# Where the softmax sums of the memory rows are formed, and which engines copy the second half of the values

## The chip, the core and the metric

The kernel runs on one core of a Trainium2 chip. The metric is the device time in microseconds (us) of one execution, as a median over runs. The engines are TensorE (PE, with its weight loads shown apart as PEld), VectorE (DVE), ScalarE (ACT), GpSimd (POOL) and SyncE (SP, which issues transfers).

## The reference, cut to what matters

The network is A, B, A, B with residuals and layer norms. A is attention with a recurrent memory, B a gated MLP with a mixing matrix over tokens. The change lies in A:

```python
for s in range(n_seg):                        # 2048 tokens in 64 segments of 32
    h = concat([mem, xs], axis=1)             # 8 memory rows + 32 token rows
    q, k, v = h @ Wq, h @ Wk, h @ Wv          # 32 heads of 128
    p = softmax(where(mask, q @ k.T * scale, -1e9))
    o = (p @ v) @ Wo
    mem = o[:, :8]                            # carried to the next segment
    outs.append(o[:, 8:])
```

Each segment needs the memory that the one before it made, so the 64 segments of a block follow each other. All 12 inputs come in bfloat16.

## The kernel before, in words

`a_block` runs one attention block and is called twice, so there are 128 segments in all. Its nested function `segment` emits one segment; the order of PE, DVE and ACT instructions is the order in which the code writes them (`manual_schedule`), and each engine works through its own list in that order. The framework adds the semaphores between engines. Where the code knows that two accesses don't touch each other, it says so itself (`declare_no_dep`, in `other_bank` and in `fold`).

The 32 heads are worked in two halves, r = 0 and r = 1, of 16 heads. In PSUM a tile of 128 partitions x 2 x 512 floats fills two banks. The tiles `att`, `attO[0]` and `attO[1]` are such pairs of banks; `accA` and `accB` are single banks. In the course of a segment they hold different things under different names:

- `att` holds psQ, then the scores psS of both halves, then psT, the sums over the softmax of the token rows.
- `attO[0]` holds psK and the first half's values, then psO[0]: the outputs of half 0 before they are normalised (columns 0 to 319 of each bank).
- `attO[1]` holds psO[1]: the outputs of half 1 (columns 0 to 319), sums in columns 320 to 383, and pw, the second part of the output projection, in columns 384 to 511.
- `accB` holds psV (the second half's values, psW in the code), then px, the first part of the output projection.

The stretch around the change, in the order of the code (lines of the profile):

1. `v_mm(1, ...)` (L762) forms the values of half 1 in four steps of four matmuls, one for each quarter of the contraction. The scores of half 1 (L1113, L1117) stand after the second of them.
2. `exps` (L1122, ACT) writes S, and `close` (L1125, DVE) multiplies it by the mask into E, where the rows of the contraction are split in two groups g of 64 partitions.
3. `sums_zero` (L1136): 16 matmuls form the sums of half 0 for the 8 memory rows, in columns 224 to 351 of the scores' first bank. Each multiplies E by the constant `half`, whose ones cover one group of 64 rows, and writes 32 partitions; they stand between the third and the fourth value step.
4. `inverse(r)` on ACT takes the logarithm of such sums (L1179) and then exp of its negative (L1180), which gives 1/sum in Rm. For half 0, ACT's copy of the values from psV (L1226) stands between the two.
5. `fill()` puts in PE work that doesn't belong to the segment: products for the next block of 128 tokens, or parts of earlier output rows (here L964 or L762).
6. `pv(0)` (L1162, L1165) forms the outputs of half 0, `sums_tokens` (L1154) the sums for the token rows of both halves, `sums_one` (L1145) the memory sums of half 1 with four matmuls, and `pv(1)` the outputs of half 1. These use 64 rows and all 128 columns of the array.
7. `memory_out(0)` (L1183, DVE) multiplies the memory rows of psO[0] by Rm into uT for 16 heads. `spare1` puts in other DVE work, a second `fill()` other PE work.
8. `inverse(1)`, then `memory_out(1)` for the other 16 heads.
9. `wo_pairs` (L945) is the output projection of the first 16 heads into px, `wo_rest` (L952) that of the others into pw. From these the memory of the next segment is built (`fold`, L1049 on ACT and L1053 on DVE, `build_hA`, L1060 and L1062).

Of the kernel before, what the change touches and what calls it, by code (L numbers as in the profile page):

```python
# [7 lines left out]
BF16 = mybir.dt.bfloat16  # L8
# [6 lines left out]
P = 128  # L15
# [52 lines left out]
def _consts(ctx, tc, c, b_sp, between):  # L68
    nc = tc.nc
    cp = ctx.enter_context(tc.tile_pool(name="consts", bufs=1))  # L70
    bsp = cp.tile([P, 16], F32, name="bsp")
    tctx = ExitStack()
    tmp = tctx.enter_context(tc.tile_pool(name="consts_tmp", bufs=1))
    maskf = tmp.tile([P, 224], F32, name="maskf")
    nc.gpsimd.memset(maskf[:], 1.0)
    fourth = tmp.tile([P, 4, 32], F32, name="fourth")
    nc.gpsimd.memset(fourth[:], 0.0)
    nc.gpsimd.affine_select(out=fourth[:], in_=fourth[:], compare_op=ALU.not_equal, fill=1.0,
                            base=0, pattern=[[-1, 4], [-4, 32]], channel_multiplier=1)
    own = maskf[:, 160:224].rearrange("p (i q) -> p i q", i=4)  # L80
    is_own = tmp.tile([P, 4, 1], F32, name="is_own")
    nc.vector.tensor_reduce(out=is_own[:], in_=fourth[:], op=ALU.max, axis=mybir.AxisListType.X)
    nc.vector.tensor_copy(own, is_own[:].to_broadcast([P, 4, 16]))
    between()
    for q in range(0, P, 32):
        blk = maskf[q:q + 32, 0:160].rearrange("p (i q) -> p i q", i=4)[:, :, 8:32]
        nc.gpsimd.affine_select(out=blk, in_=blk, compare_op=ALU.is_ge, fill=0.0, base=8,
                                pattern=[[0, 4], [1, 24]], channel_multiplier=-1)
        last = own[q:q + 32, :, 8:16]
        nc.gpsimd.affine_select(out=last, in_=last, compare_op=ALU.is_ge, fill=0.0, base=0,  # L90
                                pattern=[[1, 4], [4, 8]], channel_multiplier=-1)
    maskN = cp.tile([P, 2, 224], BF16, name="maskN")
    nc.vector.memset(maskN[:], 0.0)
    for gs in range(4):
        nc.vector.tensor_copy(maskN[32 * gs:32 * gs + 32, gs % 2, :], maskf[32 * gs:32 * gs + 32, :])
    ones = cp.tile([P, P], BF16, name="ones")
    nc.vector.memset(ones[:], 1.0)
    half = cp.tile([P, 2, 32], BF16, name="half")
    nc.vector.memset(half[:], 0.0)
    for g in range(2):  # L100
        nc.vector.memset(half[64 * g:64 * g + 64, g, :], 1.0)
    bsp_bf = cp.tile([P, 16], BF16, name="bsp_bf")

    def load_bsp():
        nc.vector.memset(bsp_bf[:], 0.0)
        nc.sync.dma_start(bsp_bf[:], b_sp.rearrange("(t p) -> p t", p=P))
        return lambda: nc.vector.tensor_copy(bsp[:], bsp_bf[:])

    c["bsp"], c["load_bsp"] = bsp, load_bsp
    tctx.close()  # L110
    c.update(maskN=maskN, ones=ones, half=half)
    return c


# [510 lines left out]
def cols_rhs(w, j, kt, cg):  # L625
    at = 2048 * (j % 2) + 512 * cg
    return w[j // 2][:, kt, at:at + 512]
# [90 lines left out]
def a_block(tc, c, rows, front, MV_in, RS_in, MV_out, RS_out, ahead, wo, S, first):  # L718
    nc = tc.nc
    NSEG = S // SEG  # L720
    NB = S // P
    scale = float(DH) ** -0.5
    maskN, ones, half = c["maskN"], c["ones"], c["half"]

    with ExitStack() as ctx:

# [33 lines left out]
        def mm_chunk(ps, lhs, rhs, kts=range(KT)):  # L760

            return [nc.tensor.matmul(ps[32 * cg:32 * cg + 32, :], lhsT=lhs(kt, cg), rhs=rhs(kt, cg), start=(kt == 0), stop=(kt == KT - 1),  # L762
                                     tile_position=(0, 32 * cg)) for kt in kts for cg in range(4)]

        def other_bank(mms, *reads):

            for m in mms:
                for r in reads:
                    tc.declare_no_dep(m.ins, r.ins, reason="another bank of the tile")
# [300 lines left out]
        def segment(s, fill, spare1, spare2, spare3, tail, loads):  # L1070
# [4 lines left out]
            VA = vsp.tile([P, 2, 4, DH], BF16, name="VA")  # L1075
# [6 lines left out]
            E = segp.tile([P, 2, 2, 224], BF16, name="E", bufs=1)  # L1082
# [9 lines left out]
            def v_mm(r, ps, kts=range(KT)):  # L1092
                return mm_chunk(ps, lambda kt, cg: hA_cur[:, kt, :], lambda kt, cg: cols_rhs(w, 4 + r, kt, cg), kts)

            def ends(q):

                return q.rearrange("p h (b e) -> p h b e", e=8)[:, :, 0:5:4, :]
# [5 lines left out]
            def heads40(q):  # L1103
                return q.rearrange("p (i q) -> p i q", q=40)
# [16 lines left out]
            def exps(r):  # L1121
                return nc.scalar.activation(out=S[:, r], in_=psS[:, r, 0:224], func=ACT.Exp, scale=scale)  # L1122

            def close(r):
                nc.vector.tensor_tensor(out=E[:, r], in0=S[:, r].unsqueeze(1).to_broadcast([P, 2, 224]), in1=maskN[:], op=ALU.mult)  # L1125

            def e_all(e, lo, hi):

                return e[:, :, 0:160].rearrange("p n (i q) -> p n i q", q=40)[:, :, :, lo:hi]

            def e_own(e, b):
                return e[:, :, 160:224].rearrange("p n (i b e) -> p n i b e", i=4, b=2)[:, :, :, b, :]

            def sums_zero(pN):

                return [nc.tensor.matmul(pN[32 * cg:32 * cg + 32, 64 * g:64 * g + 64], lhsT=half[:, g, :], rhs=e_own(E[:, 0], 0) if k else e_all(E[:, 0], 0, 8),  # L1136
                                         start=False, stop=True, tile_position=(0, 32 * cg), skip_group_check=True)
                        for k in range(2) for g in range(2) for cg in range(4)]

            def sums_one():  # L1140

                for k in range(2):
                    for g in range(2):
                        e = E[64 * g:64 * g + 64, 1]
                        nc.tensor.matmul(psO[1][:, g, 320:384], lhsT=ones[64 * g:64 * g + 64, :], rhs=e_own(e, 0) if k else e_all(e, 0, 8),  # L1145
                                         start=(k == 0), stop=True, skip_group_check=True)

            def sums_tokens(ps):

# [7 lines left out]
            def pv(r):  # L1157

                for i in range(4):
                    for g in range(2):  # L1160
                        o = psO[r][:, g, 0:320].rearrange("p (s i q) -> p s i q", s=2, i=4)[:, :, i, :]
                        nc.tensor.matmul(o, lhsT=VA[64 * g:64 * g + 64, r, i, :], rhs=E[64 * g:64 * g + 64, r, :, 40 * i:40 * i + 40],  # L1162
                                         start=(r == 0 and i == 0), stop=True, skip_group_check=True)
                for g in range(2):
                    nc.tensor.matmul(ends(heads40(psO[r][:, g, 0:320])), lhsT=VX[64 * g:64 * g + 64, j4, r, :],  # L1165
                                     rhs=E[64 * g:64 * g + 64, r, :, 160:224], start=False, stop=True, skip_group_check=True)
# [10 lines left out]
            def inverse(r, src):  # L1177
                rm = Rm[:, r]
                nc.scalar.activation(out=rm, in_=src, func=ACT.Ln)  # L1179
                return lambda: nc.scalar.activation(out=rm, in_=rm, func=ACT.Exp, scale=-1.0)  # L1180

            def memory_out(r):
                nc.vector.tensor_tensor(out=hview(uT_cur[:], r, 24, 32), in0=oview(r, 0, 8), in1=Rm[:, r].rearrange("p g (n q) -> p g n q", q=8), op=ALU.mult)  # L1183
# [21 lines left out]
            psS = att.tile([P, 2, 512], F32, name="psS")  # L1205
            scores(0)
            expd = exps(0)
# [8 lines left out]
            psW = accB.tile([P, 512], F32, name="psV")  # L1216
            v_mm(1, psW, (0, 1))
            other_bank(scores(1), expd)
            expd = exps(1)
            v_mm(1, psW, (2,))  # L1220
            pN = psS[:, 0, 224:352]
            other_bank(sums_zero(pN), expd)
            v_mm(1, psW, (3,))
            Rm = segp.tile([P, 2, 2, 64], F32, name="Rm", bufs=1)
            invert = inverse(0, pN.rearrange("p (g q) -> p g q", g=2))
            nc.scalar.copy(VA[:, 1].rearrange("p i e -> p (i e)"), psW[:])  # L1226
            invert()
            close(1)

            psO = [attO[r].tile([P, 2, 512], F32, name="psO") for r in range(2)]  # L1230
            if not begin:
                fill()
            pv(0)
            psT = att.tile([P, 2, 512], F32, name="psT")
            sums_tokens(psT)
            sums_one()
            pv(1)
            memory_out(0)
            spare1(E)
            if not begin:  # L1240
                fill()
            inverse(1, psO[1][:, :, 320:384])()
            memory_out(1)
            run(copies)
            Rt = segp.tile([P, 2, 512], F32, name="Rt", tag="Rt", bufs=1)
# [57 lines left out]
        start = nc.vector if first else nc.gpsimd  # L1303
# [138 lines left out]
        for i in range(H // 2):  # L1442
            for k in range(4):
                h = 2 * i + k % 2
                nc.tensor.matmul(pw[32 * k:32 * k + 32, :], lhsT=ends[k // 2][:, h, :], rhs=wo.head(h).rearrange("p (kt g el) -> p g kt el", kt=4, g=4),
                                 start=(i == 0), stop=(i == H // 2 - 1), tile_position=(0, 32 * k))
# [46 lines left out]
```

## Time and profile before

| What | Value |
|---|---|
| Time, median of 3 runs | 1604.93 us (1603.9 to 1605.56) |
| Profiled execution: its own time | 1610.6 us |
| Profiled execution: its span, first to last instruction | 1608.9 us |
| Granted TensorE clock | 1.000 |
| PE busy | 1579.1 us (98%), 41021 matmuls |
| DVE busy | 1070.4 us (67%) |
| ACT busy | 1052.3 us (65%) |
| POOL busy | 306.5 us (19%) |

In the profile an instruction stands under the line that issued it, with output tile, input tile, partitions x elements, and a count where several are merged. A wait line names the engine and instruction that sat idle, then what released it, then the idle time in all, how often, and the longest.

### The profile page before, as it was taken

Reading aid. Unit: us, or ns where it says so; the run is one execution under the profiler, and the core shown is the slowest. Engines: PE = TensorE matmul, PEld = TensorE weight load, DVE = VectorE, ACT = ScalarE, POOL = GpSimd, SP = SyncE. Lnnn points to the kernel's source line nnn. Section 1 sums busy time; section 2 is a strip of 40 time slices with the busy share of each in tenths; the row PEclk is TensorE's granted clock in tenths of the full one; section 3 lists DMA queues with packets and bytes.
Section 4 is the critical chain, followed back from the end, with each engine's and each line's share of the span. In section 5 each row is a group of like instructions: output and inputs, shape, how many; then the busy total and the mean of one; then the engine's idle time right before and its main releaser. Section 6 shows DMA issues by size and latency. Waiting matters only on the chain.

```text
span 1608.9 us, 90911 instructions
## 1 busy us (share of the span) xinstructions
PE 1579.1 (98%) x41021; PEld 981.3 (61%) x41046; DVE 1070.4 (67%) x3066; ACT 1052.3 (65%) x2279; POOL 306.5 (19%) x674
## 2 busy tenths in 40 slices
PE   7899999999999999999999999999999999999999
PEld 3566666666666666666656666666666766665565
DVE  4667766677777776784466666666677667768622
ACT  4677777777777777670057777777777777776400
POOL 6211111112211221320011111111122122224000
PEclk9999999999999999999999999999999999999999
DMA  9322112222311332378952212212233223426698
GB/s 364 131 57 46 40 44 44 50 42 82 80 43 40 87 86 61 106 172 175 209 162 45 48 44 50 44 47 46 73 92 73 47 72 92 97 54 178 143 194 164
DMA packets 255773, 149.67 MB, mean 93 GB/s; under 512 B 188504, under 2 KB 231104, under 8 KB 255384
## 3 DMA queue, kind: packets, MB, share of 16 engines
q1 hardware_dynamic: 241464, 97.68, 27.4%
q0 software_dynamic: 13920, 46.18, 8.9%
q8 instruction: 321, 5.26, 1.4%
q14 instruction: 68, 0.56, 0.1%
HBM read 60.21 MB, written 39.55 MB: 62 GB/s over the span
## 4 chain that ended last, share of the span: by engine, by line
PE 92%; DMA 5%; issue 1%; DVE 1%; ACT 1%; POOL 1%; SPq 0%; POOLq 0%; DVEq 0%; ACTq 0%
PE psQ L762 13%; PE psK L762 13%; PE psb L762 9%; PE pg L403 9%; PE psO L952 7%; PE px L945 7%; PE psm L762 7%; PE psV L762 7%; PE pwB L964 3%; PE psO L1162 3%; PE pz L302 3%; PE py L446 2%; PE psT L1154 2%; PE psS L1113 2%; DMA Wk_sb<-in_A_Wk_dram 1%
## 5 line engine op out<-in xcount | busy, mean ns | idle before, releaser
L762 PEld LDWEIGHTS <-hT 128*32 128x32 bf16 x12288 | 345.3, 96 | 259.2 <-DVE hT L1062 17.7
L762 PE MATMUL psV<-Wv_sb,hT 128*32 128x512 bf16 x2048 | 166.4, 379 | 0.0
L1087 ACT CAST rows<-psQ 128x512 bf16<-128x512 f32 x256 | 145.4, 588 | 23.2 <-PE psQ L762 19.4
L1183 DVE TENSOR_TENSOR uT<-psO,Rm 128x128 bf16<-128x128 f32 x256 | 74.6, 291 | 123.6 <-ACT Rm L1180 123.4
L1090 DVE STREAM_TRANSPOSE QQ<-rows 128x256 f32<-128x256 f32 x256 | 112.5, 439 | 66.2 <-ACT rows L1087 63.6
L1122 ACT ACTIVATE S<-psS 128x224 bf16<-128x224 f32 x256 | 92.2, 360 | 98.1 <-PE psS L1117 98.1
L1090 DVE STREAM_TRANSPOSE KA<-rows 128x256 f32<-128x256 f32 x256 | 113.0, 441 | 64.9 <-ACT rows L1087 62.4
L403 PE MATMUL pg<-z,wspT 128*128 128x344 bf16 x1024 | 154.3, 309 | 0.0
L762 PE MATMUL psK<-Wv_sb,hT 128*32 128x512 bf16 x2048 | 153.2, 378 | 0.0
L1186 DVE TENSOR_TENSOR uT<-psO,Rt 128x384 bf16<-128x384 f32 x256 | 139.9, 547 | 16.4 <-ACT Rt L1265 14.4
L1265 ACT ACTIVATE Rt<-Rt 128x512 f32<-128x512 f32 x256 | 147.3, 622 | 4.0
L952 PE MATMUL psO<-Wo_high,uT 128*32 128x128 bf16 x8192 | 143.0, 219 | 4.1 <-issue 2.2
L762 PE MATMUL psQ<-Wq_sb,hT 128*32 128x512 bf16 x2048 | 136.4, 379 | 0.2 <-issue 0.2
L762 PE MATMUL psQ<-Wk_sb,hT 128*32 128x512 bf16 x2048 | 136.2, 379 | 0.0
L762 PE MATMUL psK<-Wk_sb,hT 128*32 128x512 bf16 x2048 | 136.0, 379 | 0.0
L762 PE MATMUL psm<-Wq_sb,hT 128*32 128x512 bf16 x2048 | 136.0, 379 | 0.0
L945 PE MATMUL px<-Wo,uT 128*32 128x256 bf16 x3840 | 133.8, 273 | 1.3 <-issue 1.2
L952 PEld LDWEIGHTS <-uT 128*32 128x32 bf16 x8192 | 123.6, 97 | 16.2 <-issue 7.8
L403 PEld LDWEIGHTS <-wspT 128*128 128x128 bf16 x1024 | 100.1, 98 | 53.4 <-issue 0.4
L1262 ACT ACTIVATE Rt<-psT 128x1024 f32<-128x1024 f32 x127 | 130.1, 1024 | 3.1
L945 PEld LDWEIGHTS <-uT 128*32 128x32 bf16 x4096 | 104.5, 97 | 25.2 <-issue 2.6
L1044 POOL COPY KX<-old 128x128 bf16<-128x128 bf16 x128 | 65.5, 539 | 263.8 <-PE psS L1117 170.7
(224 smaller groups left out, 2892.9 us busy)
## 6 DMA issues: line engine op xcount, KB each, us to landing
o_d<-o_sb SPq DMA_DIRECT2D x126, 64.0 KB
vb_d<-front SPq DMA_DIRECT2D x31, 256.0 KB
VX<-vb_d SPq DMA_DIRECT2D x124, 64.0 KB
ln_x<-xd SPq DMA_DIRECT2D x26, 256.0 KB
y_o<-o_d POOLq DMA_DIRECT2D x22, 256.0 KB, 3.4
xd<-y_o POOLq DMA_DIRECT2D x22, 256.0 KB, 3.2
Wq_sb<-in_A_Wq_dram POOLq DMA_DIRECT2D x8, 512.0 KB, 7.1
Wk_sb<-in_A_Wk_dram POOLq DMA_DIRECT2D x8, 512.0 KB, 9.3
```

The costliest lines, as they stand in the source:

```text
L403: nc.tensor.matmul(pg[t][:, k, 0:344], lhsT=wsp[t][:, st, :], rhs=z(st, 344 * k, 344 * k + 344), start=(st == 0), stop=(st == NT - 1))
L762: return [nc.tensor.matmul(ps[32 * cg:32 * cg + 32, :], lhsT=lhs(kt, cg), rhs=rhs(kt, cg), start=(kt == 0), stop=(kt == KT - 1), tile_posi ...
L945: nc.tensor.matmul(px[at:at + 32, 0:256], lhsT=lhs[:, h, :], rhs=wo_rhs(h, slice(k + 2, None, -2) if h % 2 else slice(k, None, 2)), start= ...
L952: nc.tensor.matmul(pw[32 * cg:32 * cg + 32, :], lhsT=lhs[:, h, :], rhs=wo_rhs(h, cg), start=False, stop=(h == H - 1), tile_position=(0, 32 ...
L1044: eng.tensor_copy(KX[r][:].rearrange("p g (k i) -> p i g k", i=4), bs["KTB"][:, r].rearrange("p (i g) k -> p i g k", i=4)[:, :, :, 8 * j4: ...
L1087: return r, mms, copy(r[:].rearrange("p (n el two) -> p n el two", n=8, two=2), ps.rearrange("p (n two el) -> p n el two", n=8, two=2))
L1090: nc.vector.transpose(out=(QQ[:, j % 2, :, 0:32] if j < 2 else KA[:, j % 2]).bitcast(F32).rearrange("p n q one -> p n (q one)"), in_=r[:]. ...
L1122: return nc.scalar.activation(out=S[:, r], in_=psS[:, r, 0:224], func=ACT.Exp, scale=scale)
L1183: nc.vector.tensor_tensor(out=hview(uT_cur[:], r, 24, 32), in0=oview(r, 0, 8), in1=Rm[:, r].rearrange("p g (n q) -> p g n q", q=8), op=ALU ...
L1186: nc.vector.tensor_tensor(out=hview(uT_nxt[:], r, 0, 24), in0=oview(r, 8, 32), in1=rview(r, 0, 24), op=ALU.mult)
L1262: nc.scalar.activation(out=Rt[:], in_=psT[:], func=ACT.Ln)
L1265: nc.scalar.activation(out=rt, in_=rt, func=ACT.Exp, scale=-1.0)
```

## The change

It concerns the memory rows' sums and the copy of the second half's values.

- The sums of half 0 are no longer 16 matmuls of `half` in the scores' bank, but four matmuls of `ones`, as those of half 1 already were (`sums_memory`). They go to columns 320 to 383 of psO[1], the output banks of half 1, and stand after the first `fill()`, just ahead of `pv(0)`.
- The sums of half 1 go to the same columns of psO[0], and stand behind `pv(0)`; the token sums follow them, ahead of `pv(1)`.
- `inverse(0)` now follows the sums of half 0, with its logarithm and its exp next to each other.
- The fourth value step follows the third directly. `close(1)` comes next, and then the values are copied in two halves of 256 columns, the first by ACT, the second by DVE, both from psV.
- The constant `half` is gone.

The diff, without the lines that drop `half`:

```diff
-            def sums_zero(pN):
-
-                return [nc.tensor.matmul(pN[32 * cg:32 * cg + 32, 64 * g:64 * g + 64], lhsT=half[:, g, :], rhs=e_own(E[:, 0], 0) if k else e_all(E[:, 0], 0, 8),
-                                         start=False, stop=True, tile_position=(0, 32 * cg), skip_group_check=True)
-                        for k in range(2) for g in range(2) for cg in range(4)]
-
-            def sums_one():
+            def sums_memory(r, ps, begun):
 
                 for k in range(2):
                     for g in range(2):
-                        e = E[64 * g:64 * g + 64, 1]
-                        nc.tensor.matmul(psO[1][:, g, 320:384], lhsT=ones[64 * g:64 * g + 64, :], rhs=e_own(e, 0) if k else e_all(e, 0, 8),
-                                         start=(k == 0), stop=True, skip_group_check=True)
+                        e = E[64 * g:64 * g + 64, r]
+                        nc.tensor.matmul(ps[:, g, :], lhsT=ones[64 * g:64 * g + 64, :], rhs=e_own(e, 0) if k else e_all(e, 0, 8),
+                                         start=(k == 0 and not begun), stop=True, skip_group_check=True)
...
             expd = exps(1)
-            v_mm(1, psW, (2,))
-            pN = psS[:, 0, 224:352]
-            other_bank(sums_zero(pN), expd)
-            v_mm(1, psW, (3,))
+            v_mm(1, psW, (2, 3))
+            close(1)
+            for k, copy in enumerate((nc.scalar.copy, nc.vector.tensor_copy)):
+                copy(VA[:, 1, 2 * k:2 * k + 2].rearrange("p i e -> p (i e)"), psW[:, 256 * k:256 * k + 256])
             Rm = segp.tile([P, 2, 2, 64], F32, name="Rm", bufs=1)
-            invert = inverse(0, pN.rearrange("p (g q) -> p g q", g=2))
-            nc.scalar.copy(VA[:, 1].rearrange("p i e -> p (i e)"), psW[:])
-            invert()
-            close(1)
 
             psO = [attO[r].tile([P, 2, 512], F32, name="psO") for r in range(2)]
             if not begin:
                 fill()
+            sums = [psO[1 - r][:, :, 320:384] for r in range(2)]
+            sums_memory(0, sums[0], False)
+            inverse(0, sums[0])()
             pv(0)
+            sums_memory(1, sums[1], True)
             psT = att.tile([P, 2, 512], F32, name="psT")
             sums_tokens(psT)
-            sums_one()
             pv(1)
             memory_out(0)
             spare1(E)
             if not begin:
                 fill()
-            inverse(1, psO[1][:, :, 320:384])()
+            inverse(1, sums[1])()
             memory_out(1)
```

More of the change, by code (lines that the diff above doesn't have):

```diff
@@ L97, in _consts @@
     nc.vector.memset(ones[:], 1.0)
[L98 to L101, printed above, removed]
     bsp_bf = cp.tile([P, 16], BF16, name="bsp_bf")
@@ L110, in _consts @@
     tctx.close()
-    c.update(maskN=maskN, ones=ones, half=half)
+    c.update(maskN=maskN, ones=ones)
     return c
@@ L722, in a_block @@
     scale = float(DH) ** -0.5
-    maskN, ones, half = c["maskN"], c["ones"], c["half"]
+    maskN, ones = c["maskN"], c["ones"]
     with ExitStack() as ctx:
```

## The prediction

> **What bounds the kernel now.** I read the page first (busy shares, the chain that ended last), then the waits, then the timeline of one segment, then the same instructions in all 128 segments (64 in each attention block). The page:
>
> ```profile
> PE 1579.1 (98%) x41021; PEld 981.3 (61%) x41046; DVE 1070.4 (67%) x3066; ACT 1052.3 (65%) x2279; POOL 306.5 (19%) x674
> PE 92%; DMA 5%; issue 1%; DVE 1%; ACT 1%; POOL 1%; SPq 0%; POOLq 0%; DVEq 0%; ACTq 0%
> ```
>
> TensorE carries the chain; whatever shortens or stalls it in a segment counts 128 times. The change lies in one stretch of 3 us of each segment. The timeline of one (start, duration in us):
>
> ```profile
> 403.70 0.29 PE L1136 MATMUL psS<-E,half 128*32 128x64 bf16 x16
> 403.82 0.39 PE L762 MATMUL psV<-Wv_sb,hT 128*32 128x512 bf16 x4
> 404.04 0.39 PE L964 MATMUL pwB<-Wo,old 128*32 128x512 bf16 x4
> 404.07 0.28 ACT L1179 ACTIVATE Rm<-psS 128x128 f32<-128x128 f32 x1
> 404.14 0.39 DVE L1125 TENSOR_TENSOR E<-S,maskN 128x448 bf16<-128x448 bf16 x1 [0.21 <-ACT S L1122]
> 404.27 0.58 ACT L1226 CAST VA<-psV 128x512 bf16<-128x512 f32 x1
> 404.36 0.32 PE L1162 MATMUL psO<-E,VA 64*128 64x80 bf16 x8
> 404.58 0.45 PE L1154 MATMUL psT<-E,ones 64*128 64x512 bf16 x4
> 404.75 0.31 ACT L1180 ACTIVATE Rm<-Rm 128x128 f32<-128x128 f32 x1
> 404.87 0.22 PE L1145 MATMUL psO<-E,ones 64*128 64x64 bf16 x4
> 404.93 0.31 PE L1162 MATMUL psO<-E,VA 64*128 64x80 bf16 x8
> 405.09 0.29 DVE L1183 TENSOR_TENSOR uT<-psO,Rm 128x128 bf16<-128x128 f32 x1 [0.56 <-ACT Rm L1180]
> 405.22 0.40 PE L964 MATMUL pwB<-Wo,old 128*32 128x512 bf16 x4
> 405.33 0.28 ACT L1179 ACTIVATE Rm<-psO 128x128 f32<-128x128 f32 x1 [0.27 <-PE psO L1165]
> 405.44 1.04 PE L945 MATMUL px<-Wo,uT 128*32 128x256 bf16 x30
> 405.64 0.31 ACT L1180 ACTIVATE Rm<-Rm 128x128 f32<-128x128 f32 x1
> 405.98 0.29 DVE L1183 TENSOR_TENSOR uT<-psO,Rm 128x128 bf16<-128x128 f32 x1 [0.26 <-ACT Rm L1180]
> 406.32 0.90 PEld L952 LDWEIGHTS <-uT 128*32 128x32 bf16 x64
> ```
>
> A matmul's duration holds some 0.17 of pipeline (512 columns take 0.217 from start to start), so PE is read by starts. Three places have no slack. The token sums (L1154) start 0.058 after DVE ends E of half 1 (404.53), in all 128 segments (tenth to ninetieth percentile 0.057 to 0.059): they are released by it. The output projection wo_pairs (L945) starts as its filling work ends, and 0.06 after memory_out(0) ends (405.38). wo_rest (L952, weights at 406.32) starts 0.056 after memory_out(1) ends. The latter two hold in the 62 segments with four filling matmuls between the value sums and L945. In 64 others there are eight: L945 comes 0.22 later and both have over 0.2 us to spare. The waits name the chain behind them:
>
> ```profile
> DVE uT L1183 <- ACT Rm L1180: 123.4, 243, 1.3
> ACT Rm L1179 <- PE psO L1165: 38.8, 128, 1.9
> ```
>
> The second line says more: the logarithm of half 1 reads columns 320 to 383 of psO, written by L1145 (done at 405.09), but waits until L1165, the tail of the value sums, has written other columns. Accesses of one bank are ordered whatever their columns.
>
> **The sums of half 0.** Out go 16 matmuls of L1136, 403.70 to 403.82: 0.117. In come four like L1145, 404.87 to 404.93: 0.058. On PE alone that is 0.059 x 128 = 7.6 us saved. But the next step is now the sums of half 1, which read E of half 1 and so start at 404.59, as the token sums do today. Behind that gate stand the same matmuls in another order. PE gets to the gate earlier and waits: gain 0 (bounds: 0.006 either way from unhidden weight loads, 0.8 us).
>
> Before, the logarithm could start at 404.07, ahead of the values' copy. Now its chain is: last value step at 403.70, fill at 403.92, then as today 0.32 from fill to the first row-tiled matmul (0.11 of it a gap at the change of tile shape; there is still one such change there): sums at 404.24, second pair 0.037 later (spacing of the first L1162 pairs) plus 0.19 duration: 404.47. From PE to ACT 0.045 (L1165 to L1179; bound above 0.085, scores to L1122). Ln 404.51 to 404.79, 0.03 to Exp, which ends at 405.13; 0.03 and 0.29: memory_out(0) ends at 405.455, not 405.38. So L945 starts at 405.52 in the 62 segments, 0.08 later. Today's order hid this chain under the value and fill matmuls.
>
> ACT's value copy ahead of Ln(0) is done by then (below). pv(1) writes the bank that Ln(0) reads and waits for 404.79 + 0.057 = 404.85; it isn't due before 404.93. Price 0.
>
> **The sums of half 1 in half 0's bank.** By PE, Ln(1) could now start early, since it no longer waits for L1165. But ACT's Ln(1) and DVE's memory_out(0) now read the same bank, psO[0], and memory_out(0) stands first in program order. If two engines' reads of a bank are ordered like the other accesses, Ln(1) starts 0.035 after 405.455: 405.49 to 405.77, Exp to 406.11, memory_out(1) 406.14 to 406.435, L952 0.057 later: 406.49, not 406.33. PE itself, from 405.52, would be there at 406.39 (0.873 from L945 to L952 where nothing waits). So in the 62 segments PE loses 0.165, the 0.08 included. Queued behind Ln(1) on ACT are its Exp and, in a few segments, block copies (0.58); the next copy from px isn't due before 406.63. With eight fillers PE comes to L952 later than that gate: nothing lost.
>
> No row shows two engines reading the same partitions of a bank at once. The bounds are 0 and the order above. I take the order, because the trace orders by bank and not by columns, and because the two copies of px that do run side by side (L1049, L1053, both at 406.55) read different partitions and the code declares them independent for that reason.
>
> The Trainium skill (PSUM — Partial Sum Buffer, section "PSUM bank collisions raise a hardware error") says that two engines must not access one bank and quadrant together, reads against reads included, and that the back end adds a dependency, ScalarE against VectorE too. By that rule the order holds; no run here shows it yet.
>
> **The second values.** Now one ACT copy, 404.27 to 404.85. Then: ACT's half from 404.13 (matmuls done 404.085), 0.37 (on the line between 0.26 for 64x128, L1049, and 0.588 for 128x512, L1087), to 404.50. DVE's half reads the same bank: after ACT's, at 404.535, 0.41 (on the line between 0.28 for 128 columns, L1189, and 0.68 for 512, L1211), to 404.95. That is 0.10 later than today. The third pair of pv(1) needs it: 404.95 + 0.057 against 404.99 due, with the unhidden load 0.03 late. Bounds: 0 (DVE starting right behind E, 404.45, ends in time) and 0.09 (if all of pv(1) waited). In the 62 segments this hides before L945; in the 64 it costs 0.03. Queued behind it on DVE is memory_out(0), due 0.2 later. DVE's added 0.41 x 128 = 53 us lie in its idle 0.56 before L1183.
>
> The Trainium skill (TensorEngine Tiling, section "PSUM Bottleneck") advises both ScalarE and VectorE for emptying PSUM. By that advice both halves would be out by 404.87, in time for pv(1), and the 1.9 us below would be 0.
>
> Dropping the constant half (three memsets at the start): 0. No DMA is moved, and nothing passes a step of the SP or POOL queues.
>
> **Sum.** 62 x 0.165 = 10.2, 64 x 0.03 = 1.9: 12.1 us slower. The profiled execution took 1610.6 (span 1608.9 and 1.7 around it), so 1622.7 for it; the median of the runs is 5.7 lower: 1604.93 + 12.1 = 1617.0. A slower PE to ACT step adds 62 x 0.04 = 2.5, all of pv(1) waiting 64 x 0.06 = 3.8; some slack given back at the next scores (L1113, released by DVE) takes 1.5. This case's own range: 1613 to 1623.
>
> **Rivals.** (1) Reads by two engines are not ordered. Then Ln(1) follows Exp(0) on ACT, memory_out(1) is done before 406.1, and L952 waits for nothing, which returns today's 0.02 there. The 62 segments lose 0.08 - 0.02 = 0.06: 3.7 us, 1608.6. For it: no row shows the order. Against: ordering by bank in L1179's wait.
> (2) Not slower: the matmul count decides. If E of half 1 were there 0.09 earlier than the rows have it (404.44), PE would run through and keep 0.059 per segment: 7.6 us, 1597.3. It also needs memory_out(0) by 405.32. Against: the constant 0.058 behind E, and nothing in the change moves the scores or E.
>
> **Chances.** Forecast 0.80, rival 1 0.12, rival 2 0.05, 0.03 beyond. This kernel can tell about 0.2%, 3.2 us, from no change; rival 1 falls on both sides of that. Faster 0.06, same 0.07, slower 0.87. The range reaches down into rival 1, to 1607, and up to 1624 with both added costs.
>
> **What would show it.** Right: the half-0 Ln starts some 0.81 after the last value step starts; Ln(1) is released by DVE's memory_out(0), and so appears among ACT's waits; L952 waits for memory_out(1) in about 62 segments, 0.16 later than now; DVE's value copy starts as ACT's ends; the sums of half 1 start 0.058 after E. Wrong: Ln(1) overlapping memory_out(0) (rival 1), or the sums of half 1 starting later than 0.058 after E because PE came late (rival 2).

## The result, and the profile after

The kernel before took 1604.74 us in the comparison (median; 1603.9 to 1605.56), the changed one 1613.57 us (1610.77 to 1613.98): a ratio of 1.0052, with a 95% interval of 1.0038 to 1.0066. The change costs 8.8 us (6.1 to 10.6 by the interval). That is slower, as forecast, and inside the range, near its lower end (1613 to 1623), and 3.3 us less than the 12.1 us of the sum.

The profiled execution of after took 1613.35 us (span 1611.6, clock 1.000), that of before 1610.6, which lay 5.9 us above its own median. The two spans therefore differ by 2.7 us only, and can't be subtracted. What can be compared is the same instruction in all 128 segments, by its median distance from a fixed point of its segment. That is done below, and the sum over the segments is then held against the 8.8 us.

The page's first line and its chain:

```profile
PE 1584.7 (98%) x39510; PEld 957.3 (59%) x39510; DVE 1124.8 (70%) x3191; ACT 1050.6 (65%) x2279; POOL 305.2 (19%) x674
PE 94%; DMA 4%; issue 1%; POOL 0%; DVE 0%; ACT 0%; POOLq 0%
```

Twelve matmuls fewer in each of 128 segments are 1536. The weight loads fall by just that; the matmuls fall by 1511, since 25 of their records are missing in before (41021 matmuls to 41046 loads). PE is nevertheless busy for 5.6 us more. The records of matmuls that follow each other overlap (0.39 long, 0.217 from start to start), so a short wait between them counts as busy. DVE has 54.4 us more (the forecast had 53). The chain is PE as before, so the page says that something on PE's path is longer, and not where.

The timeline of the segment that answers to the one shown of before (start, duration; the line numbers are lower by 4 to 13). The exponentials of half 1 on ACT start at 404.84:

```profile
404.58 0.60 PE L758 MATMUL psV<-Wv_sb,hT 128*32 128x512 bf16 x8
405.01 0.39 PE L960 MATMUL pwB<-Wo,old 128*32 128x512 bf16 x4
405.23 0.39 DVE L1121 TENSOR_TENSOR E<-S,maskN 128x448 bf16<-128x448 bf16 x1
405.24 0.37 ACT L1213 CAST VA<-psV 128x256 bf16<-128x256 f32 x1
405.33 0.23 PE L1135 MATMUL psO<-E,ones 64*128 64x64 bf16 x4
405.40 0.31 PE L1152 MATMUL psO<-E,VA 64*128 64x80 bf16 x8
405.61 0.28 ACT L1169 ACTIVATE Rm<-psO 128x128 f32<-128x128 f32 x1
405.64 0.42 DVE L1213 CAST VA<-psV 128x256 bf16<-128x256 f32 x1
405.68 0.23 PE L1135 MATMUL psO<-E,ones 64*128 64x64 bf16 x4
405.73 0.45 PE L1144 MATMUL psT<-E,ones 64*128 64x512 bf16 x4
405.92 0.31 ACT L1170 ACTIVATE Rm<-Rm 128x128 f32<-128x128 f32 x1
406.00 0.37 PE L1152 MATMUL psO<-E,VA 64*128 64x80 bf16 x8
406.26 0.29 DVE L1173 TENSOR_TENSOR uT<-psO,Rm 128x128 bf16<-128x128 f32 x1 [0.19 <-ACT Rm L1170]
406.58 0.28 ACT L1169 ACTIVATE Rm<-psO 128x128 f32<-128x128 f32 x1 [0.36 <-DVE uT L1173]
406.61 1.05 PE L941 MATMUL px<-Wo,uT 128*32 128x256 bf16 x30
406.89 0.31 ACT L1170 ACTIVATE Rm<-Rm 128x128 f32<-128x128 f32 x1
407.24 0.29 DVE L1173 TENSOR_TENSOR uT<-psO,Rm 128x128 bf16<-128x128 f32 x1 [0.35 <-ACT Rm L1170]
407.58 0.90 PEld L948 LDWEIGHTS <-uT 128*32 128x32 bf16 x64 [0.20 <-DVE uT L1173]
```

Read four places. ACT's half of the values ends at 405.61 and DVE's half starts at 405.64: one after the other. (E ends at 405.62, but that is not what held DVE up: in all 128 segments its copy of the first half's values starts 0.08 before the record of the step into E ahead of it ends, while this copy starts 0.018 after it.) The sums of half 1 (the second L1135) start at 405.68, 0.06 after E is complete (405.62). The logarithm of half 1 (the second L1169) starts at 406.58, 0.03 after DVE's memory_out(0) ends (406.55), though PE had finished its input long before. And wo_rest (L948) starts at 407.58, 0.05 after memory_out(1) ends (407.53). The waits say that the third of these is the rule:

```profile
DVE uT L1173 <- ACT Rm L1170: 85.0, 243, 0.7
ACT Rm L1169 <- DVE uT L1173: 48.3, 128, 1.8
PEld L948 <- DVE uT L1173: 12.2, 61, 0.2
```

The second line has taken the place of the one where this logarithm waited for L1165: it is now released by memory_out(0) 128 times out of 128. The third gives wo_rest's wait, in 61 segments. And the copy of the second values by engine (count, then shortest, median and longest, in ns):

```profile
L1213 ACT CAST VA<-psV x128: 372/372/373, 39.9 to 1463.9; 128x256 bf16<-128x256 f32 x128
L1213 DVE CAST VA<-psV x128: 410/425/426, 41.8 to 1464.3; 128x256 bf16<-128x256 f32 x128
```

The medians over the segments, in us after the start of half 1's exponentials:

| What | before | after | later by |
|---|---|---|---|
| E of half 1 ends | 0.781 | 0.782 | 0.001 |
| first matmul of pv(0) | 0.612 | 0.562 | -0.050 |
| third pair of pv(1) | 1.249 | 1.282 | 0.033 |
| half 0's logarithm starts | 0.313 | 0.768 | 0.455 |
| memory_out(0) ends | 1.631 | 1.710 | 0.079 |
| wo_pairs starts (62 segments) | 1.699 | 1.765 | 0.066 |
| half 1's logarithm starts | 1.585 | 1.743 | 0.158 |
| memory_out(1) ends | 2.527 | 2.687 | 0.160 |
| wo_rest, first matmul (62) | 2.583 | 2.740 | 0.157 |
| wo_rest, last matmul (62) | 3.454 | 3.599 | 0.145 |
| the matmul behind it (62) | 3.535 | 3.646 | 0.111 |
| whole segment (62, four filling matmuls) | | | 0.100 |
| whole segment (64, eight filling matmuls) | | | 0.040 |

The last two rows are the median of each segment's own lengthening, and the others differences of two medians. A segment's length is taken from one start of half 1's exponentials to the next. Some segments are longer in one execution for other reasons, so the shortest ones are a check: the fifteen shortest of the 62 have a median length of 9.672 us in before and 9.775 in after, 0.103 more, and in them wo_rest's first matmul is 0.157 later, its last 0.156 and the matmul behind it 0.110. (Over all segments the difference of medians puts the last at 0.145, because the two medians fall on different segments.)

62 x 0.100 + 64 x 0.040 = 8.8 us. So the stretch accounts for the loss. That the two agree to the digit is luck: the ratio alone leaves 6.1 to 10.6 us, and in two of the experiments below the same sum lies 4 to 5 us above the time. The table also shows where the forecast was too high: 0.157 at wo_rest's first matmul (0.165 was forecast) has become 0.110 one matmul behind wo_rest and 0.100 by the end of the segment.

### The profile page after: what moved, and what is told of

The parts are those of the page before. It is cut to its first block, busy times and chain, and to the rows that moved or that the text cites. A ratio compares the mean times of both kernels' runs of the same rounds, so it can differ in the third digit from the quotient of the medians.

```text
span 1611.6 us, 87836 instructions
## 1 busy us (share of the span) xinstructions
PE 1584.7 (98%) x39510; PEld 957.3 (59%) x39510; DVE 1124.8 (70%) x3191; ACT 1050.6 (65%) x2279; POOL 305.2 (19%) x674
## 4 chain that ended last, share of the span: by engine, by line
PE 94%; DMA 4%; issue 1%; POOL 0%; DVE 0%; ACT 0%; POOLq 0%
PE psQ L758 13%; PE psK L758 13%; PE pg L399 9%; PE psb L758 9%; PE psO L948 7%; PE px L941 7%; PE psm L758 7%; PE psV L758 7%; PE pz L298 4%; PE pwB L960 4%; PE py L442 3%; PE psO L1152 2%; PE psO L1135 2%; PE psT L1144 2%; PE psS L1109 2%; DMA Wk_sb<-in_A_Wk_dram 1%
## 5 line engine op out<-in xcount | busy, mean ns | idle before, releaser
L758 PEld LDWEIGHTS <-hT 128*32 128x32 bf16 x12288 | 317.5, 97 | 271.5 <-DVE hT L1058 20.6
L1176 DVE TENSOR_TENSOR uT<-psO,Rt 128x384 bf16<-128x384 f32 x256 | 140.1, 547 | 15.5 <-ACT Rt L1254 10.6
L758 PE MATMUL psV<-Wv_sb,hT 128*32 128x512 bf16 x2048 | 150.3, 378 | 0.0
L948 PE MATMUL psO<-Wo_high,uT 128*32 128x128 bf16 x8192 | 139.8, 220 | 4.2 <-issue 2.7
L948 PEld LDWEIGHTS <-uT 128*32 128x32 bf16 x8192 | 121.1, 97 | 20.2 <-DVE uT L1173 12.2
```

Source lines behind the costliest of these rows:

```text
L948: nc.tensor.matmul(pw[32 * cg:32 * cg + 32, :], lhsT=lhs[:, h, :], rhs=wo_rhs(h, cg), start=False, stop=(h == H - 1), tile_position=(0, 32 ...
L1176: nc.vector.tensor_tensor(out=hview(uT_nxt[:], r, 0, 24), in0=oview(r, 8, 32), in1=rview(r, 0, 24), op=ALU.mult)
```

## The experiments

All ratios are to the kernel before, which ran in turn with each of them on the same chip; its time differed from chip to chip (1603.65 to 1609.13 us), so ratios are compared and not times; a figure in us behind a ratio is that ratio's excess over 1 times the median of before. "Local loss" is the median lengthening of a segment in the profiled execution, for the segments with four and with eight filling matmuls.

### Is the order of reads the main loss? The sums of half 1 back in their own bank

The theory has two parts: half 0's logarithm is late, and half 1's then waits for memory_out(0) because both read psO[0]. The rival says that this order is all of the loss. With half 1's sums in psO[1] the two read different banks.

```
             pv(0)
-            sums_memory(1, sums[1], True)
             psT = att.tile([P, 2, 512], F32, name="psT")
             sums_tokens(psT)
+            sums_memory(1, sums[0], False)
...
-            inverse(1, sums[1])()
+            inverse(1, sums[0])()
```

> The changed kernel with half 1's sums back in psO[1], behind the token sums: logarithm 1 and memory_out(0) no longer read one bank; everything else of the change stays. Theory (two prices: the late logarithm 0, carried by px into the next filling work through accB, and the ordered reads of psO[0]): logarithm 1 starts 0.045 after the tail of pv(1) again and not after memory_out(0), wo_rest starts about 0.10 earlier than in the changed kernel, but the filling work behind it then waits for px to be read, so that a segment with four fillers still loses 0.067 against before, one with eight 0.04: 62 x 0.067 + 64 x 0.04 = 6.7 us, 1611.4 us. Rival A (the ordered reads of psO[0] are all of the loss): back to 1604.7. Rival B (they cost nothing): 1613.6, as the changed kernel.

Measured: 1.0039, 1.0029 to 1.0050 (+6.3 us), local loss 0.076 and 0.041. Its waits:

```profile
ACT Rm L1169 <- PE psO L1155: 33.4, 128, 1.8
```

Half 1's logarithm is released by PE again, at 1.627 instead of 1.743, and wo_rest starts at 2.654 instead of 2.740. But of these 0.086 only 0.033 are left at the matmul behind wo_rest and 0.024 at the end of the segment (0.032 and 0.025 in the fifteen shortest): that matmul now comes 0.110 after wo_rest's last, where after has 0.046. So the order of reads costs 62 x 0.024 = 1.5 us of the 8.8; the late half 0 and the split copy cost the rest. Rival A (the order is all of the loss) falls, since 1.000 lies outside the interval. Rival B (it costs nothing) falls by the trace alone: the intervals of this ratio and of after's (1.0038 to 1.0066) overlap.

The order doesn't come from the tile Rm, into which both logarithms write: here half 1's starts 0.085 before memory_out(0), which reads the other half of Rm, has ended.

### What does the split copy do beside the rest? One copy on ACT

```
-            for k, copy in enumerate((nc.scalar.copy, nc.vector.tensor_copy)):
-                copy(VA[:, 1, 2 * k:2 * k + 2].rearrange("p i e -> p (i e)"), psW[:, 256 * k:256 * k + 256])
+            nc.scalar.copy(VA[:, 1].rearrange("p i e -> p (i e)"), psW[:])
```

> The changed kernel with one ACT copy of all 512 columns of the second values, not two halves. Theory: ACT's copy ends 0.22 later than its half did, logarithm 0 queues behind it and starts 0.12 later, and with it memory_out(0), logarithm 1 and memory_out(1); pv(1) then waits for logarithm 0 (same bank) for about 0.05 but no longer for DVE's half. Four fillers: 0.236 over before, eight fillers: 0.087 over before; 62 x 0.236 + 64 x 0.087 = 20 us, 1625 us. Rival (the two-engine copy is what costs, since its halves run one after the other): undoing it gives back 64 x 0.04 = 2.6 us or more, 1611 us.

Measured: 1.0091, 1.0074 to 1.0109 (+14.6 us), local loss 0.221 and 0.081. In the timeline the whole copy and half 0's logarithm behind it:

```profile
408.93 0.59 ACT L1212 CAST VA<-psV 128x512 bf16<-128x512 f32 x1
409.02 0.23 PE L1135 MATMUL psO<-E,ones 64*128 64x64 bf16 x4
409.41 0.28 ACT L1169 ACTIVATE Rm<-psO 128x128 f32<-128x128 f32 x1
```

The sums are done at 409.25, and with 0.04 from PE to ACT the logarithm could start at 409.29. It starts at 409.41, when ACT lets it go. (The copy's record ends at 409.52, but in before, too, the exp behind the copy starts 0.10 before the copy's record ends, in the median of the 128 segments.) In the medians it is 0.11 later than in after (0.878 against 0.768), memory_out(0) ends 0.116 later, and this is lost in the segments of four fillers (0.221 against 0.100). So the split copy saves the change 0.12 there and 0.04 with eight fillers: half 0's logarithm stands behind the copy on ACT. The sizes agree step by step, but not the total: the segments' losses add up to 18.9 us, and 14.6 were timed. Where the other 4 us come back was not found; the shortest segments are longer by the same 0.22 and 0.08, so they don't come back there.

### The split copy alone, in the kernel before

The rule of reads in order says that two halves of one bank follow each other, and so are later than one copy by ACT. The rival says that they run side by side. The Trainium skill (TensorEngine Tiling (Array Packing), section "PSUM Bottleneck") advises using both engines to empty PSUM.

```
-            nc.scalar.copy(VA[:, 1].rearrange("p i e -> p (i e)"), psW[:])
-            invert()
             close(1)
+            for k, copy in enumerate((nc.scalar.copy, nc.vector.tensor_copy)):
+                copy(VA[:, 1, 2 * k:2 * k + 2].rearrange("p i e -> p (i e)"), psW[:, 256 * k:256 * k + 256])
+            invert()
```

> The kernel before with only the copy changed: ACT copies 256 columns, DVE the other 256. Theory (two engines' reads of one bank are ordered): DVE's half starts when ACT's ends, 0.93 + 0.03 after the first sum matmul, and ends at 1.37; the third pair of pv(1), due at 1.29, starts at 1.43 or later. 0.14 x 126 = 17.6 us over before, 1622 us. Rival (reads side by side): DVE's half ends at 1.16, in time; 1604 us, no change.

Measured: 1.0094, 1.0074 to 1.0113 (+15.1 us), local loss 0.157 in segments of both kinds. The timeline of one segment:

```profile
409.00 0.37 ACT L1228 CAST VA<-psV 128x256 bf16<-128x256 f32 x1
409.09 0.32 PE L1162 MATMUL psO<-E,VA 64*128 64x80 bf16 x8
409.40 0.42 DVE L1228 CAST VA<-psV 128x256 bf16<-128x256 f32 x1
409.66 0.47 PE L1162 MATMUL psO<-E,VA 64*128 64x80 bf16 x8
```

DVE was free: its step into E ended at 409.26, and its half starts at 409.40, 0.03 after ACT's half ends at 409.37. In the medians the halves run from 0.513 to 0.885 and from 0.918 to 1.343. That is 0.83 for both, where ACT alone takes 0.585 for the whole. The second L1162 above has its eight matmuls spread over 0.47 instead of 0.31: its third pair waits for DVE's half, at 1.400 instead of 1.249. The halves are ordered, and the rival falls: followed inside one bank, the Trainium skill's advice costs 0.94%. That the shared tile VA orders the halves, and not the bank, is unlikely, since in before PE reads one half of VA (L1162, from 404.36) while ACT writes the other (404.27 to 404.85); no run copies from two banks into it. The expected 17.6 us were 2.5 too many. The local losses would even be 19.8, so here too some 5 us come back in a place that was not found.

### Half 1's sums alone, in the kernel before

```
-                        nc.tensor.matmul(psO[1][:, g, 320:384], lhsT=ones[64 * g:64 * g + 64, :], rhs=e_own(e, 0) if k else e_all(e, 0, 8),
-                                         start=(k == 0), stop=True, skip_group_check=True)
+                        nc.tensor.matmul(psO[0][:, g, 320:384], lhsT=ones[64 * g:64 * g + 64, :], rhs=e_own(e, 0) if k else e_all(e, 0, 8),
+                                         start=False, stop=True, skip_group_check=True)
...
-                                         start=(r == 0 and i == 0), stop=True, skip_group_check=True)
+                                         start=(i == 0), stop=True, skip_group_check=True)
...
+            sums_one()
             sums_tokens(psT)
-            sums_one()
...
-            inverse(1, psO[1][:, :, 320:384])()
+            inverse(1, psO[0][:, :, 320:384])()
```

> The kernel before with only half 1's sums moved to psO[0], ahead of the token sums (the sums of half 0 and the copy as before). Theory: logarithm 1 no longer waits for pv(1) but for memory_out(0), and starts 0.085 later than before (0.035 after memory_out(0) ends); wo_rest is 0.09 later in the segments with four fillers, of which the wait for px behind it gives back 0.045: 62 x 0.044 = 2.7 us, 1607.4 us; the segments with eight don't move. Rival (reads not ordered): logarithm 1 starts some 0.3 earlier than before; wo_rest comes 0.01 to 0.02 earlier, 1604 us or a little less.

Measured: 1.0017, 1.0003 to 1.0031 (+2.7 us, as expected), local loss 0.028 and 0.

```profile
ACT Rm L1179 <- DVE uT L1183: 48.6, 128, 2.0
```

Half 1's logarithm is released by memory_out(0) 128 times in the kernel before as well, once its sums lie in psO[0]. The order of reads comes with the bank, not with the rest of the change. Its price by segments, 62 x 0.028 = 1.7 us, is close to the 1.5 of the first experiment. The second pair of lines in the edit lets pv(1) begin psO[1] afresh, as the sums did while they stood there.

### Half 0's sums alone, in the kernel before

Half 0's sums in psO[1], formed by `ones`; half 1's stay in psO[1] behind the token sums, and one ACT copy stands ahead of half 0's logarithm.

```
-            v_mm(1, psW, (2,))
-            pN = psS[:, 0, 224:352]
-            other_bank(sums_zero(pN), expd)
-            v_mm(1, psW, (3,))
...
+            v_mm(1, psW, (2, 3))
             close(1)
+            nc.scalar.copy(VA[:, 1].rearrange("p i e -> p (i e)"), psW[:])
...
+            sums = [psO[1 - r][:, :, 320:384] for r in range(2)]
+            sums_memory(0, sums[0], False)
+            inverse(0, sums[0])()
             pv(0)
...
-            sums_one()
+            sums_memory(1, sums[0], False)
```

> The kernel before with only half 0's sums moved (four matmuls in psO[1] ahead of pv(0), logarithm 0 behind ACT's copy); half 1's sums stay in psO[1] behind the token sums, ACT copies all of the second values. Theory: logarithm 0 queues behind the 0.585 copy as in the kernel in which ACT copies all, so memory_out(0) ends 0.195 later than before and wo_pairs starts 0.18 later; logarithm 1 doesn't wait for memory_out(0), but px's read holds the next filling work, so four fillers lose 0.18; eight lose 0.045, by pv(1)'s wait for logarithm 0. 62 x 0.18 + 64 x 0.045 = 14 us, ratio 1.0088. Rival (fewer matmuls on PE pay once the two other edits are undone): at or below before.

Measured: 1.0107, 1.0087 to 1.0127 (+17.2 us, where 14 were expected), local loss 0.183 and 0.101. The miss has one place: the writes of half 1's sums are the first into psO[1] behind half 0's logarithm, and had been forgotten.

```profile
407.24 0.28 ACT L1169 ACTIVATE Rm<-psO 128x128 f32<-128x128 f32 x1
407.57 0.23 PE L1135 MATMUL psO<-E,ones 64*128 64x64 bf16 x4
407.63 0.32 PE L1152 MATMUL psO<-E,VA 64*128 64x80 bf16 x8
```

They wait for its read (407.52), and the logarithm is late behind ACT's full copy. In the medians they start at 1.212, 0.051 after the logarithm ends, where pv(1) starts in the changed kernel with one ACT copy, and pv(1) behind them starts at 1.269. So the segments of eight fillers lose 0.101 and not 0.045. 62 x 0.183 + 64 x 0.101 = 17.8 us agrees with the time.

With this the local losses of the three edits stand as follows (four / eight fillers; half 1's sums together with the copy were not run without half 0's):

| Edits made | Local loss |
|---|---|
| half 0's sums | 0.183 / 0.101 |
| half 1's sums | 0.028 / 0 |
| split copy | 0.157 / 0.157 |
| half 0's and half 1's sums | 0.221 / 0.081 |
| half 0's sums and split copy | 0.076 / 0.041 |
| all three | 0.100 / 0.040 |

The first and the third cost 0.183 and 0.157 one by one and 0.076 together, because each takes away what makes the other dear: with the sums of half 0 moved, its logarithm no longer stands ahead of the copy's first half on ACT (which starts at 0.396 and not at 0.513), and with the copy split, that logarithm waits for half a copy and not for a whole one.

### What came back behind wo_rest: the bank of px

The filling matmuls behind wo_rest write psb, in the same single bank (`accB`) as px. The theory: before, they waited until the fold had read px, so a late wo_rest cost nothing until that wait was used up. The lines of before, px's last read and the filling matmul behind it:

```profile
406.94 0.29 DVE L1055 TENSOR_TENSOR t<-px,cross 128x128 f32<-128x128 f32 x1
407.28 1.05 PE L762 MATMUL psb<-Wv_sb,hB 128*32 128x512 bf16 x16
```

The read ends at 407.23 and the matmul starts 0.05 later. In after wo_rest is later than that and px is free in time:

```profile
408.10 0.29 DVE L1051 TENSOR_TENSOR t<-px,cross 128x128 f32<-128x128 f32 x1
408.49 1.03 PE L758 MATMUL psb<-Wv_sb,hB 128*32 128x512 bf16 x16
```

Here the read ends at 408.39, and the matmul comes 0.10 later, behind wo_rest's last. Two kernels leave out this one read of px (the crossed half is added twice in its stead), one from before, one from after:

```
-            nc.vector.tensor_tensor(out=t1[:], in0=px[:, 0:128], in1=cross[:], op=ALU.add)
+            nc.vector.tensor_tensor(out=t1[:], in0=cross[:], in1=cross[:], op=ALU.add)
```

> The kernel before, with fold leaving out px's own half (the crossed half is added twice), so that px's bank is read last by the two copies and not by the addition behind them. The filling work behind wo_rest in the segments with four fillers writes into that bank. Theory (in the kernel before it waits for that read): wo_rest's last matmul to the next one goes from 0.081 to 0.046; 62 x 0.035 to 0.045 = 2.2 to 2.8 us faster, a ratio of 0.998. Rival (the filler isn't released by px): no change, 1.000.

> The changed kernel with the same piece of fold left out. Theory: there wo_rest comes so late that px has been read by then (0.047 from wo_rest's last matmul to the next); leaving out the read changes nothing, ratio to before 1.005 as for the changed kernel. Rival (px's read still costs there): 62 x 0.04 = 2.5 us faster than the changed kernel, 1.0035.

Measured: before without the read 0.9993, 0.9979 to 1.0006; after without it 1.0057, 1.0039 to 1.0075, against 1.0057, 1.0037 to 1.0076 for after itself, run again beside it (local loss 0.096 and 0.040):

> The changed kernel again, on the same chip and in the same rounds as the three others. All theories: a ratio of 1.005, as first measured (1.0038 to 1.0066).

The times of the first hold both the expected 0.998 and no change, and settle nothing. The trace does. Of before without the read:

```profile
404.75 0.29 DVE L1055 TENSOR_TENSOR t<-cross 128x128 f32<-128x128 f32 x1
405.05 1.04 PE L762 MATMUL psb<-Wv_sb,hB 128*32 128x512 bf16 x16
```

The addition ends at 405.04 and the matmul starts at 405.05, not 0.05 behind it. In the median of the 62 segments the step from wo_rest's last matmul to the next shrinks from 0.091 to 0.046 (and the segment by 0.051), and nothing changes in the 64. (The expectation's 0.081 was the difference of two medians; the step taken in each segment has the median 0.091.) In after it is 0.046 with and without the read. In before the matmul stands 0.045 to 0.060 behind the end of the read in 48 of the 62 segments, in after in 8. So in before the bank of px held PE up for some 0.045 in 48 of the 62 segments, and in after it mostly doesn't.

### Can the gate behind E be moved? The scores of half 1 earlier

In after, all work behind the gate waits for E of half 1. If the scores stood one value step earlier, E and the gate should come earlier. Three kernels: this in after, this in before, and a mixture.

```
-            v_mm(1, psW, (0, 1))
+            v_mm(1, psW, (0,))
             other_bank(scores(1), expd)
             expd = exps(1)
-            v_mm(1, psW, (2, 3))
+            v_mm(1, psW, (1, 2, 3))
```

> The changed kernel with the scores of half 1 one value step earlier (behind the first step, not the second), so that E of half 1 is ready some 0.12 before the sums of half 1 want it today. Theory: PE then starts those sums as it gets there, 0.08 earlier than now, but pv(1) waits all the same, first for logarithm 0 and then for DVE's half of the values, and memory_out(0) comes no earlier: no gain, ratio to before 1.0055, as the changed kernel. Rival (rival 2 of the prediction: E of half 1 alone keeps PE from what the 12 matmuls save): 0.06 x 126 = 7.6 us faster than the changed kernel, ratio 1.001.

In before the same, with the second step joined to the third:

```
-            v_mm(1, psW, (0, 1))
+            v_mm(1, psW, (0,))
...
-            v_mm(1, psW, (2,))
+            v_mm(1, psW, (1, 2))
```

> The kernel before with the scores of half 1 one value step earlier. Theory: the token sums no longer wait for E; segments with eight fillers gain 0.018, those with four nothing (memory_out(0) and px hold them): 64 x 0.018 = 1.2 us, ratio 0.9993, less than can be told from no change; the trace shows it or not. Rival (E holds every segment): 126 x 0.02 = 2.5 us, 0.9985.

The mixture has the change only in segments with eight fillers, with 384 columns of the copy on ACT and 128 on DVE, and the order of before in the others:

```
+            if not wide:
+                pN = psS[:, 0, 224:352]
+                other_bank(sums_zero(pN), expd)
...
+            else:
+                v_mm(1, psW, (3,))
+                close(1)
+                nc.scalar.copy(VA[:, 1, 0:3].rearrange("p i e -> p (i e)"), psW[:, 0:384])
+                nc.vector.tensor_copy(VA[:, 1, 3], psW[:, 384:512])
```

> A version that uses the change only where it has cover: in the segments with eight fillers the four-matmul sums in the other half's bank, with the scores of half 1 one value step earlier and the copy split 384 columns (ACT) to 128 (DVE); in those with four the sums and copy as before. Theory: pv(1) of the former ends 0.04 earlier than before (DVE's 128 columns are done at 1.23 after the last value step starts, the fourth pair starts at 1.29, not 1.33), and the late memory_out(0) and (1) stay covered by the eight fillers: 64 x 0.04 = 2.5 us faster than before, ratio 0.9985. Rival (something else in those segments is late: logarithm 0's bank, or the reads of psO[0]): 1.000 or above.

Measured: 1.0149 (1.0130 to 1.0167), 1.0082 (1.0066 to 1.0099) and 1.0084 (1.0066 to 1.0101). All three missed, and the traces of all three show one reason. Here the second:

```profile
405.67 0.45 DVE L1090 STREAM_TRANSPOSE KA<-rows 128x256 f32<-128x256 f32 x1 [0.35 <-ACT rows L1087]
405.84 0.39 PE L762 MATMUL psV<-Wv_sb,hT 128*32 128x512 bf16 x4
406.17 0.17 PEld L1113 LDWEIGHTS <-KA 128*32 128x32 bf16 x16 [0.44 <-DVE KA L1090]
```

The scores need the last transpose of the keys, which ends at 406.12. PE is at them 0.217 after the value step's start, at 406.06, and stands until 406.17. In before the scores start 0.136 (median) after this transpose; put earlier by a whole step they start 0.054 after it, in all three kernels (tenth to ninetieth percentile 0.053 to 0.054). From the first value step to the second, with the scores between, it is 0.495: 0.217 for the step, 0.15 for the scores (406.17 to 406.32), and the other 0.13 is PE standing. 128 times that is 17 us, and the second kernel lost 13. E comes only 0.083 earlier, measured from the first value step: the place of the scores had no more slack than that, and the expectations had not taken it into account. So these runs don't test what an earlier gate would bring, and no version beat the kernel before.

## Why the prediction was right, and where it was off

**The gate of the sums.** "Gain 0": right. Twelve matmuls fewer bring nothing, because half 1's sums start 0.052 after E (tenth to ninetieth percentile 0.052 to 0.053; 0.058 was said), and E comes at the same 0.78 as before. pv(0) begins 0.050 earlier and PE then waits. Rival 2 (the matmul count decides) is excluded by this row.

**The late logarithm of half 0.** Right. It starts 0.81 after the last value step starts, as said, and memory_out(0) ends 0.079 later (0.08). wo_pairs follows 0.054 behind it and comes 0.066 later. With half 1's sums at home this part, with the split copy in it, costs 0.076 in the 62 segments (rival 1 had 0.06 for it).

**The order of the reads.** Right, and shown in four ways: half 1's logarithm starts 0.033 after memory_out(0) (0.035 was taken from another pair of engines) in 128 of 128 segments; it does so in before when only its sums move; it no longer does when they stay at home; and DVE's half of the copy starts 0.032 after ACT's. Rival 1 (reads not ordered) falls, although the time of 8.8 us alone would stand between it (3.7) and the forecast (12.1). The Trainium skill (PSUM — Partial Sum Buffer, section "PSUM bank collisions raise a hardware error") says that the compiler's back end adds a dependency between two engines' accesses to one bank and quadrant, reads included. The traces agree, with these numbers. In every program here such reads are in order, so no run shows what the chip does with reads that aren't.

**The copy.** Halves of 0.372 and 0.425 (0.37 and 0.41 were said), one after the other; pv(1)'s third pair follows DVE's half by 0.057 and comes 0.033 late (0.03). What it costs in the 64 segments is 0.040 (0.03): 0.6 us more than the sum had.

**The term that was off: 62 x 0.165.** wo_rest's first matmul is 0.157 late, so the working up to that point holds to 0.008. But the sum then carried this number to the end of the segment unchanged, and there it is some 0.100. The difference lies right behind wo_rest. wo_rest itself takes as long as before from its first matmul to its last (medians of 0.858 and 0.859), but the step to the next matmul is 0.046 and not 0.091. That 0.045 is the wait for px's bank, which before cost as much in 48 of the 62 segments and which a late wo_rest hides; the two kernels without that read show it. About 0.01 more comes back later in the segment; this was read off the medians and not tested. 62 x (0.165 - 0.100) is 4.0 us too many, 64 x 0.01 too few: 12.1 - 4.0 + 0.6 = 8.7. The prediction did allow 1.5 us for slack "given back at the next scores". It comes back, but earlier, at the first matmul behind wo_rest, and 62 x 0.045 = 2.8 us of it. The chain of waits had been followed to the instruction that is late, and not past it to the next one that had been waiting for something else.

**What the edits are worth together.** The prediction costed the split copy at 1.9 us. That holds in this place only: alone it costs 15 us, and here it even saves 0.12 us in a segment with four fillers, since the logarithm that the change puts behind ACT's copy would otherwise be later still.

## What to carry to other kernels

A delay at an instruction is worth, at the end of the stage, only what the next waits don't swallow: after finding what is late, read what the following instruction on the bound engine was waiting for before, and subtract that. When sums, outputs and copies share a PSUM bank, list the readers by engine as well as the writers, because in all these runs two engines' reads of the same partitions of a bank followed each other in program order, and splitting one copy over two engines inside a bank made it longer. Before moving a step earlier, look up how long its inputs have been ready there, since that is all that the move can gain.

## What the runs showed of the hardware that was not expected

- Two engines emptying one bank, their reads in order, are slower than one: 0.372 + 0.032 + 0.425 = 0.83 us for 128x512 in halves on ACT and DVE, 0.585 us on ACT alone. The order was foreseen; that it turns a shared copy into a loss of 0.94% of the kernel was not.
- A filling matmul that opens a new tile in a bank waits for the last read of the old one, 0.054 us after the read ends, even where that read takes 128 of the bank's columns: some 0.045 us of PE time in 48 of 62 segments in the kernel before.
- Edits of one segment don't add: two that cost 17.2 and 15.1 us alone cost 6.3 us with the third edit's bank left as it was.
